# One displaced activation slot instead of three, in attention with two feed-forward layers

## The chip, the core and the metric

The kernel runs on one core of one Trainium2 chip. The metric is the device time of one execution in microseconds (us). Engines are named as in the profile: PE (TensorE matmuls), PEld (its weight loads), DVE (VectorE), ACT (ScalarE), POOL (GpSimd) and SP (the queue that issues most DMAs).

## What is computed

Attention with normalised q and k over 4 batches of 12 heads, 448 tokens and 64 dimensions, and then two feed-forward layers on 1792 tokens, all in float32.

```python
def _attn_ref(q, k, v, g_q, g_k):
    q_n, k_n = (rmsnorm(q, g_q), rmsnorm(k, g_k))
    scores = 1.0 / np.sqrt(q.shape[-1]) * np.matmul(q_n, k_n.transpose(0, 1, 3, 2))
    attn = np.exp(scores - np.max(scores, axis=-1, keepdims=True))
    attn = attn / (np.sum(attn, axis=-1, keepdims=True) + 1e-09)
    return np.matmul(attn, v)

def _moe_ref(x, w_in, w_out):            # w_in 768x2048, w_out 2048x768
    r = np.maximum(x @ w_in, 0.0)
    return r * r @ w_out

def _moe2_ref(x, w_gate, w_val, w_out):  # 768x1536, 768x1536, 1536x768
    g = x @ w_gate
    return g * (1.0 / (1.0 + np.exp(-g))) * (x @ w_val) @ w_out
```

## The kernel before

**Precision.** Each float32 operand of the feed-forward layers is kept as two halves, a rounded one and the rest, in one tile of two rows of 448 (activations) or 384 (weights) numbers a partition. A product of such operands is three matmuls (`mm3`, L368): rounded weights by the rounded activations, rounded weights by the rest, rest of the weights by the rounded activations. Every one of them goes through line 366, has a 128x128 weight operand and 448 columns of activations.

**Stages.** Up to some 380 us the attention runs, with part of layer 1 filling PE's gaps. Then a few ordinary products of layer 1 follow. From 445 us to the end PE works through 14 **passes**, numbered 0 to 13, written out by `all_passes` (L1465): 0 to 5 belong to layer 1, 6 to 13 to layer 2. A pass takes a pair of batches and 1 (passes 0, 1), 2 (2 to 5) or 3 (6 to 13) **units**, 34 in all. A unit (`unit`, L1503) computes two blocks of the layer by Strassen's seven products of half-sized blocks, in this order: p1 (operand b11), p6 (t2), p2 (b21), p5 (t1), p3 (b22), p7 (t3), p4 (t4). Each product runs over three thirds of its depth, each third one activation tile and three matmuls, so a product is nine matmuls in a row and a unit 63. After the last unit of a pass come its **output sums** (`outputs`, L1649), matmuls into the tiles y: 72 in passes 0 and 1, 144 in passes 2 to 5, 108 in passes 6 to 13.

**Order.** The order of all instructions on all engines is made by a planner in the kernel (costs and due times, `simulate`) that knows nothing of addresses.

**Activation slots.** b11, t1, b22, b21, t2, t3 and t4, three thirds each, are 21 tiles. They lie in 21 slots: q0 to q18 of the pool `xq`, and two more of another pool. An ordinary slot is [128, 2, 448] float32: two halves of 1792 bytes (28 x 64) a partition. The pool starts at a multiple of 64 bytes with a 32-byte tile `off`, after which comes q0. A second 32-byte tile, `on`, is laid in front of the slot that `even_from` names. Slots in `padded` have rows of 456 numbers, 1824 bytes (28.5 x 64), and use 448 of them.

So, before the change, q0 lies 32 bytes off multiples of 64 with both halves ("displaced as a whole"), q1 with its first half only (the rounded one), and q2 with its second half only (the rest). q3 to q18, the two other slots, the weights and the operands of the output sums lie on multiples of 64. In q0 all three matmuls of a third read a displaced half; in q1 the first and the third; in q2 the second.

**Which tile is in which slot.** Slots are handed out from the free list in the order in which the products gave them back (`load_pair`, L1339; `product`, L1507). A load serves one or two passes. Followed through the nine loads, q0 always holds the first third of b11, the first operand that a unit reads. The others hold (third counted from 0):

| passes | 0 | 1, 2 | 3, 4 | 5 | 6 | 7, 8 | 9, 10 | 11, 12 | 13 |
|---|---|---|---|---|---|---|---|---|---|
| q1 | t1/0 | t1/2 | b21/2 | b11/2 | b22/0 | t3/0 | t3/1 | t2/1 | b11/1 |
| q2 | b22/0 | t3/0 | t3/1 | t2/1 | b11/1 | t1/0 | t1/2 | b21/2 | b11/2 |

The pool `xq` takes the room of the attention's tiles when the attention is done; q0, q1 and q2 lie where its tile `ring` was.

Of the kernel before, what the change touches and what calls it, by code (L numbers as in the profile page):

```python
# [10 lines left out]
F32R = mybir.dt.float32r  # L11
# [6 lines left out]
B, H, S, D = 4, 12, 448, 64  # L18
# [72 lines left out]
def attention_two_ffn_kernel(  # L91
# [290 lines left out]
    def tile_at(where, shape, dtype, name):  # L382
        return where[0].tile(shape, dtype, tag=where[1], name=name)
# [902 lines left out]
    xq = ctx.enter_context(tc.tile_pool(name="xq", bufs=1, side="right", reuse_waits="tile"))  # L1286
    xq.tile([128, 8], F32, tag="off", name="off")
    x_slots = [(xq, f"q{i}") for i in range(X_SLOTS)]
    padded, even_from = {"q1", "q2"}, "q2"

    def x_tile(slot, name):
        nonlocal even_from
        if slot[1] == even_from:
            xq.tile([128, 8], F32, tag="on", name="on")
            even_from = None
        if slot[1] in padded:
            return tile_at(slot, [128, 2, S + 8], F32R, name)[:, :, :S]
        return tile_at(slot, [128, 2, S], F32R, name)
    x_free, w_free, io_free = x_slots + [(xp, "x6"), (xp, "x7")], [], [(xq, "io0")]

# [38 lines left out]
    def load_pair(n):  # L1339
        layer, p, _ = passes[n]  # L1340
        X = pair_x[n] = {}
        rank = starts[n] - 2
        cells = [{} for _ in range(3)]
        plain = [set() for _ in range(3)]
        for kk in range(3):
            spawn(differences(n, kk, X, cells[kk], plain[kk], rank), rank)
        for names in (("b11", "t1", "b22", "b21"), ("t3", "t2", "t4")):
            for kk in range(3):
                for name in names:
                    yield lambda: x_free  # L1350
                    slot = x_free.pop(0)
                    cells[kk][name] = x_tile(slot, f"{name}_{n}_{kk}"), slot
                    if name in QUARTER:
                        h, j = QUARTER[name][0], kk + 3 * QUARTER[name][1]
                        spawn(fetched(layer, PAIRS[p][h], j, cells[kk][name][0], name, plain[kk]), rank)
# [440 lines left out]
```

## Time and profile before

| | |
|---|---|
| median of 3 timed runs | 1217.95 us (1217.49 to 1221.06) |
| the profiled execution | 1215.34 us, span 1213.6 us |
| PE busy | 1191.9 us (98% of the span), 6336 matmuls |
| PEld, DVE, ACT, POOL busy | 84%, 77%, 59%, 26% |
| granted TensorE clock | full in all of the page's 40 slices |

A matmul's duration in the trace, 0.37 us, spans more than the interval from its start to the next one's start, since matmuls overlap. Starts are the better measure of pace. In a piece of the chain of waits, length over count is the mean interval. In the timeline a product is one row of nine matmuls, and its time is the start of the next row minus its own.

### The profile page before, as it was taken

The numbers are of one execution on the slowest core, as the hardware profiler recorded it, in microseconds if no ns is written. First come the engines' busy times: TensorE is split into PE (matmuls) and PEld (weight loads), VectorE is DVE, ScalarE is ACT, GpSimd is POOL, SyncE is SP. The second block draws the span as 40 slices with busy tenths as digits, with TensorE's granted clock in tenths as the row PEclk, the third lists the DMA queues.
The fourth block names the chain that finished last, engine by engine and source line by source line (L and its number), as shares of the span: only waits on it lengthen the run. The fifth ranks groups of instructions, "written<-read, shape, count | busy, mean of one in ns | idle before, by whom it ended". The sixth has DMA issues, their size and how long they took to land.

```text
span 1213.6 us, 19924 instructions
## 1 busy us (share of the span) xinstructions
PE 1191.9 (98%) x6336; PEld 1015.3 (84%) x6336; DVE 939.4 (77%) x1905; ACT 711.0 (59%) x1574; POOL 316.2 (26%) x441
## 2 busy tenths in 40 slices
PE   8889999999999999999999999999999999999998
PEld 6656667777777898999999999999999999999997
DVE  7999987886775599597678788887978587846854
ACT  6999878776686467564456664645454435433410
POOL 4444454343120004321223230100040404130200
PEclk9999999999999999999999999999999999999999
DMA  7566667567545757978787986579776977785514
GB/s 222 172 202 193 180 202 234 177 211 219 171 144 166 259 192 161 239 180 218 170 241 152 270 178 215 197 211 287 242 151 191 226 218 152 206 213 148 179 31 152
DMA packets 147228, 235.88 MB, mean 194 GB/s; under 512 B 23137, under 2 KB 126706, under 8 KB 147122
## 3 DMA queue, kind: packets, MB, share of 16 engines
q1 hardware_dynamic: 129842, 207.07, 54.1%
q0 software_dynamic: 17280, 27.53, 14.4%
q8 instruction: 50, 0.82, 0.3%
q14 instruction: 56, 0.46, 0.1%
HBM read 152.80 MB, written 81.73 MB: 193 GB/s over the span
## 4 chain that ended last, share of the span: by engine, by line
PE 85%; DVE 6%; ACT 5%; DMA 2%; issue 1%; SPq 0%; POOL 0%; DVEq 0%; ACTq 0%
PE p L366 36%; PE y L366 28%; PE o L936 4%; PE ya L366 4%; PE sc L765 3%; PE h_a L366 3%; PE pt L896 2%; ACT ring L807 2%; DVE sc L793 1%; ACT turned_p L258 1%; PE h L366 1%; PE h_lead L366 1%; PE pt L894 1%; PE pt L891 1%; DVE ring L831 0%
## 5 line engine op out<-in xcount | busy, mean ns | idle before, releaser
L366 PE MATMUL y<-s,o_split 128*128 128x448 f32 x1584 | 328.6, 368 | 0.3 <-ACT yw L1699 0.3
L366 PEld LDWEIGHTS y<-s,o_split 128*128 128x128 f32 x1584 | 297.0, 188 | 29.6 <-ACT yw L1699 0.6
L366 PE MATMUL p<-t,s_split 128*128 128x448 f32 x918 | 203.9, 366 | 0.0
L1535 DVE TENSOR_TENSOR u<-p,u 128x448 f32<-128x448 f32 x204 | 124.4, 619 | 92.7 <-PE p L366 85.9
L366 PEld LDWEIGHTS p<-t,s_split 128*128 128x128 f32 x918 | 172.4, 188 | 14.9
L366 PE MATMUL p<-b,a_split 128*128 128x448 f32 x612 | 135.5, 366 | 0.0
L807 ACT ACTIVATE ring<-sc,m,rms 128x448 f32<-128x448 f32 x168 | 124.1, 745 | 9.7 <-DVE m L794 6.6
L366 PEld LDWEIGHTS p<-b,a_split 128*128 128x128 f32 x612 | 114.9, 188 | 9.7
L1699 ACT COPY yw<-y 128x448 f32<-128x448 f32 x144 | 73.4, 538 | 66.1 <-PE y L366 62.8
L258 ACT COPY turned_p<-pt 128x512 f32<-128x512 f32 (+2 forms) x167 | 87.9, 541 | 22.6 <-PE pt L896 20.2
L793 DVE TENSOR_REDUCE sc<-sc 128x2 f32<-128x896 f32 (+1 forms) x96 | 93.6, 975 | 7.4 <-PE sc L765 6.4
L1708 POOL DMA_DIRECT2D y1d<-yw x72 | 63.3, 1118 | 109.7 <-ACT yw L1699 107.4
L936 PE MATMUL o<-turned_p,v 128*64 128x448 f32 x384 | 79.6, 545 | 1.6 <-ACT turned_p L258 1.0
L258 ACT CAST t<-t_plain 128x448 fp32r<-128x448 f32 x108 | 60.9, 567 | 28.1 <-DVE t_plain L1145 19.0
L896 PE MATMUL pt<-ident,ring 128*128 128x128 f32 x432 | 70.6, 274 | 2.7 <-ACT ring L807 2.2
L366 PE MATMUL ya<-sa,hi_out 128*128 128x448 f32 x216 | 70.8, 385 | 0.0
L366 PE MATMUL h_a<-x,hi_in 128*128 128x448 f32 x216 | 68.8, 384 | 0.0
L366 PE MATMUL p<-t,a_split 128*128 128x448 f32 x306 | 68.5, 367 | 0.0
L366 PE MATMUL p<-b,s_split 128*128 128x448 f32 x306 | 68.1, 367 | 0.0
L1165 ACT ACTIVATE raw_a<-raw_a 128x384 f32<-128x384 f32 x67 | 37.7, 566 | 47.4 <-DMA raw_a<-in_w_gate_dram 21.2
L896 PEld LDWEIGHTS pt<-ident,ring 128*128 128x128 f32 x432 | 52.5, 140 | 12.4 <-ACT ring L807 2.7
L366 PEld LDWEIGHTS p<-t,a_split 128*128 128x128 f32 x306 | 57.4, 188 | 5.5
(182 smaller groups left out, 2190.0 us busy)
## 6 DMA issues: line engine op xcount, KB each, us to landing
raw_o<-in_w_out_dram SPq DMA_DIRECT2D x44, 384.0 KB
y1d<-yw POOLq DMA_DIRECT2D x72, 224.0 KB, 6.4
s_d<-a SPq DMA_DIRECT2D x68, 192.0 KB
s_split<-s_d SPq DMA_DIRECT2D x68, 192.0 KB
kq<-in_kq_p_dram SPq DMA_DIRECT2D x23, 480.0 KB
y2d<-yw POOLq DMA_DIRECT2D x48, 224.0 KB, 7.9
b<-y1d SPq DMA_DIRECT2D x45, 224.0 KB
a_d<-a SPq DMA_DIRECT2D x51, 192.0 KB
```

The source lines that it names most:

```text
L258: e.copy(out, src)
L366: return {"P": 203}, lambda e: e.matmul(ps, lhsT=w, rhs=x, start=first, stop=last), 0
L765: e.matmul(parts[t][:, :S], lhsT=q[a][d, bass.ts(i % 4, 128)], rhs=k[c][d], start=(p == 0), stop=(p == len(passes) - 1),)
L793: e.tensor_reduce(out=top, in_=sc, axis=AX.X, op=ALU.max, negate=True)
L807: yield {"A": 704}, lambda e: e.activation(out=slot(i), in_=parts[t][:, :S], func=ACTF.Exp, bias=m[:, t:t + 1], scale=rq[:, i:i + 1], accu ...
L891: e.transpose(pieces[:, :, j], p[:, bass.ts(j, 128)] if j < 3 else ends, ident)
L896: e.transpose(ps[:, bass.ts(j + (i > 3), 128)], p[:, bass.ts(j, 128)], ident)
L936: e.matmul(o[64 * h:64 * h + 64], lhsT=v[:, 4 * h + j], rhs=turned_p[:, 4 * h + j if j < 3 else 3], start=(j == 0), stop=(j == 3),)
L1165: e.activation(out=high.bitcast(F32), in_=high.bitcast(F32), func=ACTF.Copy, scale=2.0 ** -112)
L1535: return {"V": 535}, lambda e: e.tensor_tensor(out=out, in0=ps, in1=b, op=ALU.add)
L1699: yield {"A": 424}, lambda e: e.copy(y, ps)
L1708: yield {"G": POOL_DMA}, lambda e: e.dma_start(out=dst, in_=y, accum_op=ALU.add), 2 * 128 * S * 4, POOL_LATER, True
```

## The change

Slots q1 and q2 lose their padded rows and become ordinary slots, and the tile `on` is laid in front of q1 instead of q2. q0 keeps its displacement of 32 bytes in both halves, and nothing else is displaced. Since the pool is 128 bytes smaller and ends where it did, q0 begins 128 bytes higher than before, q1 160 and q2 64 bytes higher; q3 and all that follows stay where they were.

```diff
-    padded, even_from = {"q1", "q2"}, "q2"
+    even_from = "q1"
 
     def x_tile(slot, name):
         nonlocal even_from
         if slot[1] == even_from:
             xq.tile([128, 8], F32, tag="on", name="on")
             even_from = None
-        if slot[1] in padded:
-            return tile_at(slot, [128, 2, S + 8], F32R, name)[:, :, :S]
         return tile_at(slot, [128, 2, S], F32R, name)
```

## Rows read from the trace of the kernel before

**Rows 1.** The page: the span, and the chain that ended last by engine.
```profile
span 1213.6 us, 19924 instructions
...
PE 85%; DVE 6%; ACT 5%; DMA 2%; issue 1%; SPq 0%; POOL 0%; DVEq 0%; ACTq 0%
```

**Rows 2.** Busy time by stretch: passes 0 to 13, 2 to 13, sums of pass 9.
```profile
core 0: us, PE busy (x) PEld busy (x) DVE busy (x) ACT busy (x) POOL busy (x), PEclk, DMA share, GB/s
445.41:1207.68 762.27, 762.00 (x3719) 697.58 (x3718) 576.67 (x1089) 368.70 (x745) 158.51 (x168) 1.00 0.73 195
...
501.63:1209.68 708.05, 708.04 (x3456) 648.46 (x3455) 528.59 (x996) 331.17 (x667) 136.83 (x145) 1.00 0.72 194
...
944.78:966.67 21.89, 21.89 (x109) 20.29 (x109) 12.71 (x26) 10.49 (x22) 10.66 (x12) 1.00 0.93 219
```

**Rows 3.** Chain of waits: start us, us, what; passes 1, 7 and 9.
```profile
473.81 12.85 PE p L366 x63
486.66 14.97 PE y L366 x72
...
823.29 22.31 PE y L366 x108
...
944.78 21.89 PE y L366 x108
```

**Rows 4.** Timeline of PE: start, us, what; p1, p7, p4, p1 in pass 7.
```profile
784.64 1.99 PE L366 MATMUL p<-b,a_split 128*128 128x448 f32 x9
...
793.77 2.01 PE L366 MATMUL p<-t,s_split 128*128 128x448 f32 x9
795.61 2.02 PE L366 MATMUL p<-t,a_split 128*128 128x448 f32 x9
797.47 1.99 PE L366 MATMUL p<-b,a_split 128*128 128x448 f32 x9
```

**Rows 5.** Timeline of PE: p6, p2 and p5 in pass 11.
```profile
1028.60 2.00 PE L366 MATMUL p<-t,s_split 128*128 128x448 f32 x9
1030.43 2.02 PE L366 MATMUL p<-b,a_split 128*128 128x448 f32 x9
1032.28 2.02 PE L366 MATMUL p<-t,s_split 128*128 128x448 f32 x9
```

**Rows 6.** Timeline of PE: p1 and p6, p3 and p7, pass 9, unit 2.
```profile
919.01 2.00 PE L366 MATMUL p<-b,a_split 128*128 128x448 f32 x9
920.84 1.99 PE L366 MATMUL p<-t,s_split 128*128 128x448 f32 x9
...
926.32 2.02 PE L366 MATMUL p<-b,s_split 128*128 128x448 f32 x9
928.18 2.00 PE L366 MATMUL p<-t,s_split 128*128 128x448 f32 x9
```

**Rows 7.** Timeline of PE: p4 of unit 2, pass 13, and the next p1.
```profile
1172.98 2.02 PE L366 MATMUL p<-t,a_split 128*128 128x448 f32 x9
1174.84 2.00 PE L366 MATMUL p<-b,a_split 128*128 128x448 f32 x9
```

**Rows 8.** Timeline of PE: first p1 and p6 of pass 2, last of pass 12.
```profile
501.46 1.99 PE L366 MATMUL p<-b,a_split 128*128 128x448 f32 x9
503.29 0.97 PE L366 MATMUL p<-t,s_split 128*128 128x448 f32 x4
...
1113.82 1.99 PE L366 MATMUL p<-b,a_split 128*128 128x448 f32 x9
1115.65 0.57 PE L366 MATMUL p<-t,s_split 128*128 128x448 f32 x2
```

**Rows 9.** Timeline of PE: p1 and p4 of pass 0, start of its sums.
```profile
445.41 1.99 PE L366 MATMUL p<-b,a_split 128*128 128x448 f32 x9
...
456.43 2.02 PE L366 MATMUL p<-t,a_split 128*128 128x448 f32 x9
458.29 10.12 PE L366 MATMUL y<-s,o_split 128*128 128x448 f32 x48
```

**Rows 10.** Timeline of DVE in the output sums of pass 7.
```profile
829.36 0.62 DVE L1140 TENSOR_TENSOR s<-u,s 128x448 fp32r<-128x448 f32 x1 [0.27 <-ACT s L258]
```

## The prediction

> **What bounds the kernel now.** I read the page first: in the chain that ended last PE holds 85% of the span [rows 1]. The reader is to see that only matmul time can move much. Then the busy time by stretch: from the first product that reads an activation slot to the last matmul PE is busy for 762.00 of 762.27 us, at a granted clock of 1.00, so the clock hides nothing and almost nothing is waited for [rows 2]. That stretch is a queue of equal matmuls (128x128 weights, 448 columns), and its time is their number times the interval from one start to the next. Their durations overlap and don't help; intervals come from the chain of waits (a piece's length over its count) and from the timeline (differences of starts).
>
> Read so, the same work has **two cadences**. The output sums of pass 9 take 21.89 us for 108 matmuls, 202.7 ns each; those of pass 7 take 22.31 us, 206.6 ns each [rows 3]. Same instruction, shapes and count, nobody waiting: 4.0 ns, 2%. I call them short and long. All operands of the output sums are ordinary in both passes, so it isn't the address being read that differs: the stream carries a state.
>
> **Where the state changes.** The timeline of pass 7 goes product by product, nine matmuls each. The first five products of a unit (p1, p6, p2, p5, p3) take 9.13 us, 1.83 each; p7 takes 1.84 and p4 1.86 [rows 4]. Nine short matmuls are 9 x 0.20267 = 1.82 us, nine long ones 1.86. The next p1 is short again, so something in p1 turns long into short, and something in p7 turns it back. In pass 7 the wholly displaced q0 is read by the first three matmuls of p1, and q1, whose first half is displaced, by the first three of p7. Pass 11 is the test, since there q1 is in p6 and q2 in p2: p6 takes 1.83 us and p2 already 1.85 [rows 5]. The turn has moved with the slots. In unit 2 of pass 9, p3 takes 1.86 right after q2 at the end of p5 [rows 6].
>
> Over all 34 units: 26 end in the long cadence, p4 at 1.86 us (first in pass 0 [rows 9], last in pass 13, unit 2 [rows 7]), each with a half-displaced tile read since q0's three matmuls. In 26 units p1 reads no half-displaced tile; in all of these, 18 that arrive long and 8 that arrive short, the stream is short after q0. The first and the last that arrive long are in passes 2 and 12, both 1.83 us [rows 8]; unit 2 of pass 9 arrives short and takes 1.83 [rows 6]. I saw no turn from short to long among ordinary operands; the sums of pass 9 run 108 in a row without one [rows 3].
>
> **The change, part by part.** (1) q1 and q2 become ordinary: in each of 34 units two tiles of three matmuls, the only thing seen to turn short into long. (2) q0 stays displaced as a whole and first in p1 of every unit, so what turns long into short stays. (3) q0, q1 and q2 shift by 128, 160 and 64 bytes. They lie inside the attention stage's tile ring before and after, so the first loads wait for the same tile. No instruction, transfer or queue position is added or removed.
>
> What (1) is worth is the time spent above the short cadence. Passes 2 to 13 have 3456 matmuls and take 708.05 us [rows 2]; at 202.67 ns they would take 700.43, so 7.62 us. Pass 0's products take 12.88 us (445.41 to 458.29 [rows 9]) and pass 1's 12.85 [rows 3], against 63 x 0.20267 = 12.77: 0.19. Pass 1's sums take 14.97 us [rows 3] against 14.59; part of this 0.38 can be a wait, and I count 72 x 4.0 ns = 0.29. Pass 0's sums hold most of PE's 0.27 us of idle time and are counted at nothing. Together **8.1 us**, all on the path.
>
> What is left of it:
> - q0's three matmuls on arrival in the short cadence. Their p1 takes 1.83 us in pass 9 [rows 6] against 1.82; with the rows' rounding 0 to 0.02 us, 34 times, so 0 to 0.7. I take 0.01 as read: **0.3 us**.
> - A wait may leave the stream long until the next q0. Nearest are the starts of the sums, where data come late: in pass 7 DVE ends a half of s at 829.98 us, 6.7 us into the sums that read it [rows 10, 3]. No row tells which cadence follows a wait. For three such passes (1, 3, 7) the price is 0 to (72 + 144 + 108) x 4.0 ns = 1.3 us; between ends with no nearer row I take the middle, **0.65**.
> - A faster PE meets its suppliers earlier. In pass 9's sums, which run short, DVE is busy for 12.71 of 21.89 us and PE doesn't stop, with the DMA engines at 0.93 [rows 2]. Bound 0 to 0.4 us (about what the products of one pass gain); that row is nearest, so 0.
>
> What comes before pass 0 and after the last matmul stays. Sum: 8.1 - 0.3 - 0.65 = 7.15 us. The profiled execution took 1215.34 us (span 1213.6 [rows 1]) and would take 1208.2; the median of the timed runs, 1217.95, is 2.6 above it, and I carry that over: **1210.8 us**.
>
> **Rivals.**
> - The operand's address plays no part, the cadence goes by something else and returns as before: 1217.95. Against it: the turn follows q1 and q2 from p7 to p6 and p2 [rows 4, 5]. For it: 4 ns is little, and one execution is all I have. [...]
> - q0's three matmuls turn short into long when they arrive at a step of the short rhythm that the eight units didn't show. At worst every second unit is long: in passes 2 to 5 that is unit 2 and the sums, 4 x 207 matmuls, in passes 6 to 13 half of 8 x 297. 2016 x 4.0 ns = 8.1 us are lost, which is what is won: 1217.95.
> - **Slower:** q0, now 128 bytes higher, no longer turns long into short (its lifting is known at the old address alone). The first wait that leaves the stream long then leaves it so to the end: at worst 3726 x 4.0 ns = 14.9 us above the short cadence instead of 8.1, so +6.8 and 1224.7. It is slower from the point where more than 8.1/14.9 = 54% of the matmuls run long. Against it: q1 and q2, at other offsets, act on the stream too [rows 4 to 6].
>
> **How the numbers follow.** Forecast 0.85; address without part 0.06; q0 turning both ways 0.05; slower 0.04. About 0.3%, 3.7 us, is what a measurement of this kernel can tell from no change. The forecast's case lies beyond that: faster 0.85, the same 0.06 + 0.05 = 0.11, slower 0.04. Range: at best all 8.1 us, and 0.6 for a median at the low end of the runs (1217.49 was seen): 1209.2. At worst 8.1 - 0.7 - 1.3 - 0.4 = 5.7 us, and 1.8 for a median of runs that reach 1221.06: 1214.0. The other cases, 0.15 in all, stay outside.
>
> **What would show it.** Right: the sums of all passes from 2 on at 21.9 us for 108 and 29.2 for 144; p7 and p4 at 1.82 or 1.83; p1 no worse than 1.84. Wrong: sums that still take 22.3 after a p1 of 1.83 (something else turns the stream), units that alternate between a p4 of 1.82 and of 1.86 (second rival), long throughout (third), or a pass that is long from a wait on, which is the 0.65.

## The result and the profile after

The changed kernel is **slower**: 1224.66 us in the median of 6 runs (1221.97 to 1227.5) against 1217.72 us for the kernel before in the same comparison. The ratio on record is 1.0051 with a 95% interval of 1.0031 to 1.0071 (the two medians alone give 1.0057), so the loss of half a percent is small but clear of the noise. The forecast was 1210.8 us, faster. What came is the third rival's outcome, priced at 1224.7.

Page of the changed kernel, span and chain:

```profile
span 1223.8 us, 19924 instructions
...
PE 79%; DVE 6%; ACT 6%; DMA 5%; issue 1%; SPq 1%; POOL 0%; DVEq 0%; ACTq 0%; POOLq 0%
```

Busy time by stretch (columns as in [rows 2]), passes 2 to 13 after the change:

```profile
505.92:1219.95 714.03, 714.02 (x3456) 648.39 (x3455) 530.40 (x996) 330.76 (x667) 136.79 (x145) 1.00 0.72 192
```

The same 3456 matmuls take 714.03 us where they took 708.05 [rows 2], again at the full granted clock and with PE never idle: 206.6 ns each, the long cadence throughout. The profiled executions differ by 1225.62 - 1215.34 = 10.3 us. Of this, passes 2 to 13 are 5.98 us; passes 0 and 1 are 0.03 (56.22 us from 445.41 to 501.63 before [rows 9, 2], 56.25 from 449.67 to 505.92 after). The other 4.26 us lie ahead of pass 0. The change moves nothing there, and two executions of one kernel below (experiments 10 and 11) differ ahead of pass 0 by 3.5 us, so I take this part for scatter. That is argued, not shown: in experiment 11 the granted clock was 0.99 before 440 us, in the changed kernel it was 1.00. The medians, 6.9 us apart, are nearer to 6.0 than to 10.3.

Chain of waits after (start us, us, what), to hold beside [rows 3]:

```profile
478.04 13.01 PE p L366 x63
491.05 14.87 PE y L366 x72
505.92 26.03 PE p L366 x126
531.95 29.76 PE y L366 x144
...
913.14 39.04 PE p L366 x189
952.18 22.32 PE y L366 x108
```

The sums of pass 9 took 21.89 us [rows 3] and now take 22.32, like those of every pass from 2 on: 29.76 for 144, 22.32 for 108. Products too: 39.04 us for 189 is 206.6 ns each. The timeline of PE after the change, pass 0 and then pass 7, shows where that begins and that it no longer ends:

```profile
449.67 2.01 PE L366 MATMUL p<-b,a_split 128*128 128x448 f32 x9
451.52 2.02 PE L366 MATMUL p<-t,s_split 128*128 128x448 f32 x9
453.38 2.02 PE L366 MATMUL p<-b,a_split 128*128 128x448 f32 x9
...
790.26 2.02 PE L366 MATMUL p<-b,a_split 128*128 128x448 f32 x9
792.12 2.02 PE L366 MATMUL p<-t,s_split 128*128 128x448 f32 x9
```

In pass 0, p1 takes 1.85 us and p6 1.86: q0's own three matmuls have turned a short stream long. In pass 7, p1 takes 1.86 where it took 1.83 [rows 4]: the stream arrives long, and q0 leaves it so. To see single matmuls I also took the differences between their starts in the trace. Short is a repeating rhythm of about 202, 203, 199, 207, 202 ns, long is 206, 207, 207. Of the 34 units after the change, 32 arrive long and all of these leave q0 long; the two that arrive short (passes 0 and 1) leave it long too. Between these two the stream gets short once more, in the sums of pass 0: one interval there is 210 ns among 207s, and what follows is short. In the kernel before PE halts around that same matmul (280 and 305 ns from start to start), and there too a long stream is short afterwards.

**Addresses.** From the kernel as built, every ordinary operand that PE reads in the passes (activation slots, weights, operands of the sums) starts at remainder 192 when its address in the partition is divided by 256; 1792 is 7 x 256, so the second half of a tile has the remainder of the first. q0 begins at byte 159264 before and at 159392 after, that is at remainder **32** and then at **160**. Both are 32 off a multiple of 64. "Keeps its displacement" was true of that measure alone. By the remainders of 256, the two halves of q1 lay at 32 and 64 before the change and those of q2 at 128 and 160, so both halves of each were off 192, not one. The experiments ask what the measure is.

### The profile page after: what moved, and what is told of

Its sections match the earlier page's. It is cut to its first block, busy times and chain, and to the rows that moved or that the text cites. A ratio compares the mean times of both kernels' runs of the same rounds, so it can differ in the third digit from the quotient of the medians.

```text
span 1223.8 us, 19924 instructions
## 1 busy us (share of the span) xinstructions
PE 1199.5 (98%) x6336; PEld 1016.8 (83%) x6336; DVE 941.3 (77%) x1905; ACT 710.9 (58%) x1574; POOL 315.5 (26%) x441
## 4 chain that ended last, share of the span: by engine, by line
PE 79%; DVE 6%; ACT 6%; DMA 5%; issue 1%; SPq 1%; POOL 0%; DVEq 0%; ACTq 0%; POOLq 0%
PE p L366 36%; PE y L366 28%; PE ya L366 4%; PE o L936 3%; PE h_a L366 2%; ACT ring L807 2%; PE sc L765 2%; PE pt L896 2%; DVE sc L793 2%; ACT turned_p L258 1%; DMA nat<-in_k_n_dram 1%; PE h L366 1%; DMA rkb<-rkd 1%; DMA zb<-zd 1%; DMA kq<-in_kq_p_dram 1%
## 5 line engine op out<-in xcount | busy, mean ns | idle before, releaser
L936 PEld LDWEIGHTS o<-turned_p,v 128*64 128x64 f32 x384 | 29.1, 136 | 41.9 <-issue 31.1
```

Source lines behind the costliest of these rows:

```text
L936: e.matmul(o[64 * h:64 * h + 64], lhsT=v[:, 4 * h + j], rhs=turned_p[:, 4 * h + j if j < 3 else 3], start=(j == 0), stop=(j == 3),)
```

## The experiments

All edits are relative to the changed kernel unless said otherwise. The tile `on` lies between q0 and q1, so its size sets where q0 begins, and nothing else moves. q0 **lifts** when it turns a long stream short, and **throws** when it turns a short one long. A time from one execution has no interval; beside experiments 5 to 8 one execution of the kernel before took 1220.56 us. There the reading rests on the cadences in the trace.

**1. q0 back at its old address**, q1 and q2 ordinary as in the change.

```diff
-            xq.tile([128, 8], F32, tag="on", name="on")
+            xq.tile([128, 40], F32, tag="on", name="on")
```

> The changed kernel with 128 bytes more between q0 and q1: q0 alone is displaced and lies where it lay before the change, at remainder 32 of 256, while all else that PE reads in the passes lies at remainder 192 of 256 (in the changed kernel q0 is at 160). Theory A (what q0's three matmuls do to the cadence goes by where q0 lies within 256 bytes): lifted at the first p1 and short from there, sums of pass 9 in 21.9 us, median 1210.8 us (1209 to 1214). Theory B (q0 lifted only with the half-displaced q1 and q2 in the stream): long as in the changed kernel, sums 22.3 us, median 1224.7. Theory C (the cadence isn't set by addresses but differs by execution): anything, and profiled units of both kinds.

Measured: median 1212.59 us (1208.38 to 1214.15, 8 runs), against 1217.51 for the kernel before beside it: ratio **0.9947**, 95% interval 0.9927 to 0.9968. The profiled execution took 1208.38 us (span 1206.6). Chain of waits, from the sums of pass 0 to those of pass 2:

```profile
468.87 5.21 PE y L366 x24
474.09 12.77 PE p L366 x63
486.86 14.95 PE y L366 x72
501.81 25.55 PE p L366 x126
527.36 29.18 PE y L366 x144
```

The last 24 sums of pass 0 run long (5.21 us; short ones take 5.13, see experiment 10), and then the products of pass 1 take 12.77, the short 63 x 202.7 ns. The timeline shows the lift in p1: 1.82 us, and 1.83 after it.

```profile
473.93 1.99 PE L366 MATMUL p<-b,a_split 128*128 128x448 f32 x9
475.75 1.99 PE L366 MATMUL p<-t,s_split 128*128 128x448 f32 x9
477.58 1.99 PE L366 MATMUL p<-b,a_split 128*128 128x448 f32 x9
```

Busy time by stretch, passes 2 to 13:

```profile
501.81:1202.74 700.93, 700.91 (x3457) 648.61 (x3455) 530.45 (x996) 330.19 (x667) 138.26 (x145) 1.00 0.72 196
```

700.93 us for what takes 714.03 in the changed kernel: 128 bytes, one slot and 13 us. This version beats both kernels. So parts (1) and (2) of the forecast hold at the old address, and the address is what the forecast left out.

**2. q0 alone moved.** The kernel before (q1 and q2 padded, at their own addresses), with a tile of 128 bytes between q0 and q1, which puts q0 at remainder 160. Relative to the kernel before:

```diff
+        if slot[1] == "q1" and even_from:
+            xq.tile([128, 32], F32, tag="gap", name="gap")
         if slot[1] == even_from:
```

> The kernel before with q0 alone moved 128 bytes down, from remainder 32 to 160 of 256; q1 and q2 keep their padded rows and their addresses. Theory A: q0 no longer lifts; p1 of passes 2 to 4, 7, 8 and 12 arrives long and leaves long (1.85 or 1.86 us for the next product instead of 1.82), what q1 and q2 do to a long stream is all that is left, and the time is 1221 to 1226 us. Theory B: q1 and q2 are there, so as before, 1217.7 us and p6 at 1.82.

Measured: 1215.38 us, one execution. What q0 does to a long stream was as theory A has it; the time, outside its 1221 to 1226, was not. Timeline of PE, pass 2, unit 1 (p1, p6, p2, p5, p3, p7, p4, next p1):

```profile
502.89 2.02 PE L366 MATMUL p<-b,a_split 128*128 128x448 f32 x9
504.74 2.02 PE L366 MATMUL p<-t,s_split 128*128 128x448 f32 x9
506.60 2.02 PE L366 MATMUL p<-b,a_split 128*128 128x448 f32 x9
508.46 2.01 PE L366 MATMUL p<-t,s_split 128*128 128x448 f32 x9
510.31 1.98 PE L366 MATMUL p<-b,s_split 128*128 128x448 f32 x9
512.13 2.01 PE L366 MATMUL p<-t,s_split 128*128 128x448 f32 x9
513.98 2.02 PE L366 MATMUL p<-t,a_split 128*128 128x448 f32 x9
515.84 2.02 PE L366 MATMUL p<-b,a_split 128*128 128x448 f32 x9
```

The unit arrives long. q0 in p1 leaves it long (p6 and p2 1.86 us), where the kernel before took 1.83 for the first p1 of this pass [rows 8]. But then p3 takes 1.82: q1, read by the last third of p5, has lifted the stream, and q2 in p7 throws it back (p7 1.85, p4 1.86). By single starts, q1 met a clearly long stream in 24 units and left it short in all 24. Its halves lie at remainders 32 and 64. So q1 was not only what turns short into long; it took over the lifting that q0 had lost, and the time stayed near that of the kernel before. With q1 ordinary, as in the change, no slot is left that lifts.

Two more things about 160 can be read here. q0 begins at byte 159136, 256 bytes below its place in the changed kernel, and meets a long stream with the same three intervals as there (205, 207, 201 ns). And it doesn't throw every short stream: in the passes where p1 has no other displaced tile, 16 units arrive short, of which q0 leaves 12 long and 4 short; these four all arrive at one and the same step of the short rhythm, the twelve at others.

**3. No displaced slot at all**: q0 at remainder 192 too.

```diff
-    xq.tile([128, 8], F32, tag="off", name="off")
+    xq.tile([128, 16], F32, tag="off", name="off")
-    even_from = "q1"
+    even_from = None
```

> The changed kernel with no displaced slot at all: q0 too lies at remainder 192 of 256, like everything else. Theory A, if only a displaced read or a wait can turn the stream: it arrives short at pass 0 and stays short until a wait turns it, so between 1210 us (never) and 1225 us (at the first sums). If ordinary operands hold the short cadence only after a lift, 1224.7. Theory B: the same as the changed kernel, 1224.7.

Measured: median 1214.32 us of 10 runs; ratio 0.9989 (0.9952 to 1.0026) without the highest of them, no difference from the kernel before that can be told. But the single times lie in two groups: six from 1208.37 to 1216.64, and four from 1224.46 to 1226.86. The profiled execution, 1211.61 us, was of the lower group and ran short from pass 0 to the end (701.70 us for passes 2 to 13). What the upper group is was left to runs 10 and 11.

**4. q0 at remainder 64**, a multiple of 64 and so no longer displaced by the measure that the change uses.

```diff
-            xq.tile([128, 8], F32, tag="on", name="on")
+            xq.tile([128, 32], F32, tag="on", name="on")
```

> The changed kernel with q0 at remainder 64 of 256: on a multiple of 64, so ordinary by the kernel's own measure, but 128 bytes off the 192 at which all else lies. If the 32 bytes against multiples of 64 matter, q0 does nothing and the time is that of no displaced slot. Theory A (position within 256 bytes): q0's triple has a rhythm of its own, other than nine matmuls in 1.82 or 1.86 us all through, and may lift; 1210 to 1225 us.

Measured: 1218.25 us, one execution. Timeline of PE, pass 3: p1 and p6 of unit 1, then p4 of it and p1, p6 of unit 2.

```profile
560.05 2.00 PE L366 MATMUL p<-b,a_split 128*128 128x448 f32 x9
561.89 2.02 PE L366 MATMUL p<-t,s_split 128*128 128x448 f32 x9
563.75 2.02 PE L366 MATMUL p<-b,a_split 128*128 128x448 f32 x9
...
571.19 2.02 PE L366 MATMUL p<-t,a_split 128*128 128x448 f32 x9
573.05 1.99 PE L366 MATMUL p<-b,a_split 128*128 128x448 f32 x9
574.87 1.38 PE L366 MATMUL p<-t,s_split 128*128 128x448 f32 x6
```

q0 acts at a multiple of 64. It lifts: the second p1 arrives long (p4 1.86) and takes 1.82. And from some steps of the short rhythm it throws: after the first p1 (1.84) p6 takes 1.86. Over all passes the 12 units that arrive long all leave it short; of the 22 that arrive short, 11 stay short and 11 go long. This is the second rival's behaviour, at another address than the rival meant; that this one execution came near its price (1217.95) is luck.

**5 and 6. The ordinary slots of the pool moved to remainder 64**, with q0 at 32 (5) and at 160 (6). Weights and operands of the sums stay at 192.

```diff
-    even_from = "q1"
+    even_from, padded = "q1", []
...
+        if slot[1] == "x6" and not padded:
+            padded.append(xq.tile([128, 32], F32, tag="pad", name="pad"))
```

Experiment 6 also makes the tile `on` 40 numbers wide instead of 8.

> The changed kernel with all ordinary slots of the pool moved 128 bytes down, from remainder 192 to 64 of 256; q0 lies at 32, its address before the change; weights and the operands of the sums stay at 192, and so do the two slots of the other pool, which are now the odd ones. Theory A1 (what counts is q0's distance from the other activation operands, 160 down or 96 up in the kernel before, 32 down in the changed one): here 32 down, so q0 doesn't lift, a unit that arrives long leaves p1 long. Theory A2 (its distance from the weights, its own remainder): 32 as in the kernel before, so it lifts, p6 follows at 1.82 us.

> The same with q0 at remainder 160, as in the changed kernel, 160 down (96 up) from the other slots at 64. Theory A1: lifts as in the kernel before. Theory A2: arrives long and leaves long. In this run and the one before it the two other slots and the step from the products (64) to the sums (192) may turn the stream as well; times between 1208 and 1227 us, and the verdict is read from the triples of q0 that arrive long.

Measured: 1217.04 and 1211.37 us, one execution each. As a test of time this one failed: products whose operands lie at 64 run in rhythms of their own (p6 at 204.9 ns a matmul in many units), so what follows q0 can't be set beside the other kernels. What can be is q0's own three matmuls in units that arrive long, by single starts (ns):

```
q0 at  32: experiment 1 (others at 192)  205, 204, 202     experiment 5 (others at 64)  204, 204, 203
q0 at 160: the change   (others at 192)  205, 207, 201     experiment 6 (others at 64)  205, 207, 201
```

These three intervals go with q0's own place, not with its distance from the neighbouring activation slots. Its distance from the weights, which stay at 192 in all of these, isn't told apart from its own place. Whether the stream is lifted isn't shown by them: in experiment 6 a p1 that arrives long takes 1.82 us, where the changed kernel took 1.85, so with its neighbours at 64 a q0 at 160 did not leave the stream long as theory A2 expected. What follows therefore holds for operands that all lie at 192.

**7. q0 at remainder 96**, again 32 off a multiple of 64.

```diff
-            xq.tile([128, 8], F32, tag="on", name="on")
+            xq.tile([128, 24], F32, tag="on", name="on")
```

> The changed kernel with q0 at remainder 96 of 256, 32 bytes off multiples of 64 like 32 and 160, all else at 192. Theory A says only that it acts in its own way. If the lift falls off evenly from 32 (lifts from any step) over 64 (lifts, but not from every step of the short rhythm) to 160 (never), 96 lifts from long and throws out from some steps, 1212 to 1222 us; if it goes by remainder 32 of 128, not as 32, since 160 has the same remainder and didn't lift.

Measured: 1223.13 us, one execution. Busy time by stretch, passes 2 to 13, and the timeline of pass 0:

```profile
503.62:1217.44 713.82, 713.81 (x3457) 648.39 (x3455) 528.87 (x996) 331.41 (x667) 137.52 (x145) 1.00 0.72 193
```

```profile
447.39 2.01 PE L366 MATMUL p<-b,a_split 128*128 128x448 f32 x9
449.24 2.02 PE L366 MATMUL p<-t,s_split 128*128 128x448 f32 x9
451.10 2.02 PE L366 MATMUL p<-b,a_split 128*128 128x448 f32 x9
```

As at 160: the stream arrives short in pass 0, q0 throws it (p1 1.85, p6 1.86), and it stays long to the end. "32 off a multiple of 64" covers 32, 96 and 160, of which only the first lifts. A lift that falls off evenly from 32 over 64 to 160, the first case of the expectation, is ruled out.

**8 and 9. q0 at remainder 0**, one execution and then twelve.

```diff
-            xq.tile([128, 8], F32, tag="on", name="on")
+            xq.tile([128, 48], F32, tag="on", name="on")
```

> The changed kernel with q0 at remainder 0 of 256, a multiple of 64, 64 bytes up (192 down) from all else at 192. If only offsets that are no multiple of 64 count, as the kernel's own measure has it: no effect, the stream keeps the cadence it arrives in. Theory A: next to 32, it lifts, 1208 to 1216 us.

> The changed kernel with q0 at remainder 0 of 256, timed now in many executions. In the profiled execution at this place q0 kept every stream short, but every stream arrived short, so whether it also lifts a long one was not to be seen. If q0 at 0 lifts (theory A: a fixed property of the place), every execution lies at 1207 to 1213 us, as with q0 at 32 (median 1212.6). If it only keeps and doesn't lift (theory B), the executions fall into two groups as they do without any displaced slot: some at 1208 to 1216, and about 4 in 10 at 1224 to 1227, where a wait has left the stream long and nothing turned it back.

Measured: 1208.25 us at first; then a median of 1212.87 us of 12 runs, ratio 0.998 (0.9952 to 1.0008). Both profiled executions (1208.25 and 1207.61) run short in all 34 units (the first with 701.26 us for passes 2 to 13), and every unit arrives short. The 13 times lie from 1207.61 to 1218.21 in ten executions and from 1222.02 to 1224.03 in three, which looks like the groups of experiment 3, though the gap between them is 3.8 us here and 7.8 there, and not like experiment 1, whose highest is 1214.15. At 0, q0 keeps a stream short. That it does not lift is inferred from the times and not shown, since no execution of the upper group was profiled here.

**10 and 11. The kernel of experiment 3 twice more**, to see an execution of its upper group.

> The kernel with no displaced slot once more, for one profiled execution. Its ten times lay in two groups. If the upper group is a stream left long by one wait (theory A), an execution at 1224 to 1227 us shows short sums (29.2 us for 144, 21.9 for 108) up to some wait and long ones (29.8, 22.3) in all that follows; one at 1208 to 1216 us shows short sums nearly throughout. If the upper group is something else (theory B), such as later loads, sums are short in it too and idle time or another stage is longer by some 15 us.

> The kernel with no displaced slot a third time, for one more profiled execution, with the same expectations: at 1224 to 1227 us either long sums from one wait on (theory A) or short sums and 15 us elsewhere (theory B); at 1208 to 1216 us short sums nearly throughout.

Measured: 1210.52 and 1226.78 us. The chain of waits of the first, from the sums of pass 0 on:

```profile
469.83 5.13 PE y L366 x24
474.96 12.77 PE p L366 x63
487.73 14.79 PE y L366 x72
502.52 25.54 PE p L366 x126
528.06 29.18 PE y L366 x144
```

and of the second:

```profile
473.74 5.22 PE y L366 x24
478.96 13.02 PE p L366 x63
491.98 14.88 PE y L366 x72
```

One kernel, the same matmuls, short in one execution and long in the other. The timeline of the second shows the turn:

```profile
461.45 1.98 PE L366 MATMUL p<-t,a_split 128*128 128x448 f32 x9
463.27 10.19 PE L366 MATMUL y<-s,o_split 128*128 128x448 f32 x48
473.74 5.22 PE L366 MATMUL y<-s,o_split 128*128 128x448 f32 x24 [0.28 <-ACT yw L1697]
478.80 2.02 PE L366 MATMUL p<-b,a_split 128*128 128x448 f32 x9
480.66 2.02 PE L366 MATMUL p<-t,s_split 128*128 128x448 f32 x9
```

The last product before the sums of pass 0 is short (1.82 us). In the sums PE waits, the last time 0.28 us for ACT; the 24 sums after it run long, and so does everything to the end of pass 13, 714.03 us for passes 2 to 13 as in the changed kernel:

```profile
506.86:1220.89 714.03, 714.03 (x3456) 648.30 (x3455) 530.79 (x996) 330.82 (x667) 137.60 (x145) 1.00 0.72 192
```

So the stream can be long after a wait (in experiment 4 it is so twice more, after the waits in the sums of passes 3 and 7), and among ordinary operands, with PE never idle after it, no turn back is seen in 33 units. Experiment 1 meets the same situation (5.21 us for the last 24 sums) and is lifted by q0 in the next p1. That is what a slot that lifts is worth here: not a shorter interval, but a way back. Not every wait does it: in the profiled executions of experiments 3 and 10 PE also waits in the sums of passes 0, 1, 3 and 7, and by single starts the stream came out short each time. What decides that, the length of the wait or the step of the rhythm, I did not settle.

Together, for one slot with both halves at the same remainder and all other operands at 192 (in the rows of the kernel before and of experiment 2, all but q1 and q2):

| remainder of q0 | met long, leaves | met short, leaves | times, us |
|---|---|---|---|
| 0 (exp. 8, 9) | not seen; by the times, long (inferred) | short | 1207.6 to 1218.2, and 1222.0 to 1224.0 |
| 32 (before; exp. 1) | short (18 times before, twice in exp. 1) | short | exp. 1: median 1212.59, highest 1214.15 |
| 64 (exp. 4) | short | short or long, by the step | 1218.25 |
| 96 (exp. 7) | long | long (met once) | 1223.13 |
| 160 (the change; exp. 2) | long | long (twice in the change); long 12 times, short 4 times in exp. 2 | the change: median 1224.66 |
| 192 (exp. 3, 10, 11) | long | short | 1208.4 to 1216.6, and 1224.5 to 1226.9 |

128 and 224 weren't tried.

## Why the prediction was wrong

**What held.** The two cadences and their sizes: 202.7 and 206.6 ns carry every row above. The stake: the kernel before stood some 8 us above an all-short run, and the best version (experiment 1) lies 700.93 against 708.05 us in passes 2 to 13. Part (1): without q1 and q2, and with q0 at its old address, the stream is short after every q0, and the profiled execution took 1208.38 us where the forecast said 1208.2. The two terms left over were 0.3 us for q0's arrivals and 0.65 for waits that leave the stream long; experiment 1 shows 0.26 and 0.33 (0.08 in the sums of pass 0, 0.25 in those of pass 1). The term put at 0, a faster PE that meets its suppliers earlier, is 0.24 us there, in the sums of pass 3:

```profile
582.09 29.42 PE y L366 x144
```

That is within its bound of 0.4 in experiment 1, but not in experiment 10, where the sums of pass 7 take 1.3 us longer than short ones, with halts of PE. The median of experiment 1, 1212.59, is 1.8 us above the forecast, mostly since its timed runs lie 4.2 above its profiled execution and I carried over 2.6.

**The step that failed** is part (2) with part (3): "q0 stays displaced as a whole and first in p1 of every unit, so what turns long into short stays", and the shift by 128 bytes entered at no cost. The lifting is no property of being displaced; it belongs to a place. At remainder 32 q0 lifts, at 160 it doesn't and even throws a short stream: 700.93 us in experiment 1 against 714.03 in the changed kernel for the same passes, so the move that entered at nothing costs 13.1 us. The rows of before showed q0 at one address only, and the third rival said so ("its lifting is known at the old address alone"). What is known at one place gives no ground to expect it at another, and 0.04 was not a chance that the rows bore out.

**What I set against that rival was no argument.** "q1 and q2, at other offsets, act on the stream too": they act, but the question was whether they lift. And there the trace of before held a hint that I read past. In unit 2 of pass 9, p3 takes 1.86 us and p7 begins at 928.18 [rows 6]. p7's first third is still long, then q1 comes in its second third. The timeline of that unit goes on:

```profile
930.02 1.99 PE L366 MATMUL p<-t,a_split 128*128 128x448 f32 x9
931.84 1.99 PE L366 MATMUL p<-b,a_split 128*128 128x448 f32 x9
```

p7 takes 1.84 and p4 1.82: q1 lifted the stream in the kernel before too. So "two tiles ... the only thing seen to turn short into long" was half of what q1 does. Had I asked of every tile what it does on a long arrival, I would have had q1 (32, 64) lifting and q2 (128, 160) met long and leaving long (in 11 units by single starts, the first in p3 of pass 0) as two more points of the table, and q0's new 160 would have stood on the side that doesn't lift. The trace of before also answered what the forecast said no row tells, which cadence follows a wait. Pass 0 ends long (p4 1.86 us [rows 9]), PE waits in its sums, and the last 24 of them are short:

```profile
468.68 5.13 PE y L366 x24
```

So a stream can turn at a wait in either direction: to short here, to long in experiment 11.

**The third rival** was right in the lost lift and near in the price: +6.8 us forecast, 6.0 in the passes of the two profiled executions. That the medians lie 6.9 apart is in part luck. Its trigger was not quite right. It has a wait leave the stream long; in the profiled execution q0 itself threw it, in pass 0 and again in pass 1. That fits with all six times of the changed kernel being high, while without any displaced slot, where a wait was what threw it, five of twelve are; only one of the six was profiled, so for the others it is inferred.

**The first rival**, that the address plays no part, is refuted by experiment 1: only q0's address differs from the changed kernel, and its eight times end at 1214.15, where the six of the changed kernel begin at 1221.97. The Trainium skill, "SBUF — State Buffer", section "Specifications (TRN2)", gives 16-byte cache lines, and by these alone a place at 32 and one at 160 are alike, since both are whole numbers of lines. The rows have 700.93 and 714.03 us for them, and the measurement decides. **The second rival**, q0 turning both ways, is what q0 does at 64 (experiment 4, 1218.25 us).

**Still open**: whether the lifting goes by q0's own place or by its distance from the weights or the neighbouring slots (experiments 5 and 6 settle the last for three intervals only); whether the measure repeats every 256 bytes (32 and 160 differ, so it doesn't every 128, and 160 was met at two addresses 256 apart; no other remainder was); what happens in PE or in the memory to make two cadences; and which waits leave the stream long.

## What to carry to other kernels

When a change keeps a property ("displaced by 32 bytes") but moves the thing that has it, list every measure by which the old and the new place could differ, and give the move a price of its own. When a stream carries a state, ask of each event what it does in either state, and of the kernel what brings it back: a kernel with nothing that does so can be fast in one execution and slow in the next. Where a kernel's times lie in two groups, profile one execution of each before trusting a median.

## What the runs showed of the hardware

- One form of matmul (128x128 weights, 448 columns, new weights each time) is issued every 202.7 or every 206.6 ns, at full granted clock and with PE always busy. The long state lasted for 3456 matmuls in a row (experiment 11, passes 2 to 13), the short one as long with short waits in between (experiment 10).
- Three matmuls that read an operand at another place within 256 bytes can turn that state, and places 32 bytes apart do different things (the table). This was measured with everything else at remainder 192.
- The state can also turn at a wait of PE of a few tenths of a us, in either direction (experiment 11: 0.28 us is the last one before the stream is long; the kernel before, sums of pass 0: long to short). Not every such wait turns it (experiments 3 and 10).
- The two states are worth 13 us of some 1210 here, and 128 bytes in the place of one slot of 21 decide between them.
